# A larger share per slot for background weight preparation in the last three blocks of the first network, and a lower planned price for the scans of the last weight matrix

## The chip, the cores and the metric

The kernel runs on one core of a Trainium2 chip. The metric is the device time of one execution in microseconds (us). The engines are TensorE (PE, matmul; PEld is its weight load), VectorE (DVE), ScalarE (ACT), GpSimd (POOL) and SyncE (SP, which issues the DMAs).

## The reference

A strided-attention layer over 4 batches, 8 heads, 576 positions and head size 64 gives 2304 tokens of width 512. Two feed-forward networks follow; the weights are float64 on the host.

```python
h = x @ w_in                                # 512 -> 2048
x = (h * cos(h)) @ w_out                    # 2048 -> 512
g = x @ w_gate                              # 512 -> 1536
out = (g * sigmoid(g) * (x @ w_val)) @ w_out2   # 1536 -> 512
```

## The kernel before

**Tokens and stages.** The 2304 tokens are cut into five blocks (`BLOCKS`): three of 512 and two of 384, called blocks 0 to 4. After attention the first network runs for all five blocks, then the second.

**First network.** Each block has 16 slots, one for each 128 rows of the 2048, so there are 80 slots, 0 to 79; block 2 begins at slot 32, block 3 at 48, block 4 at 64. In a slot TensorE does `up1` (12 matmuls into one of four PSUM banks of the pool `pm`) and one or two times `down1` (12 matmuls each, for an earlier slot whose product is waiting in a queue). Every operand is split in two float16 halves, high and low, so a product is three matmuls (`mm3`, L491 to L493). The nonlinearity takes five steps, spread over three later slots: `up1_a` (ACT, L524), `up1_b` (DVE, L527), `up1_c` (ACT, L531), `up1_d` (DVE, L534), `up1_e` (ACT L538 and POOL L539). A bank is free again after `up1_d`. All engines run their instructions in the order in which they are written.

**Second network.** There are 30 slots s0 to s29, six for each block. Every slot does seven products for a pair of 128-row pieces (`multiply`, 84 matmuls of 256 columns in blocks 0 to 2), and the previous slot's two `down2` contractions with a tile of `w2` (24 matmuls of 512 columns in blocks 0 to 2). Its nonlinearity uses L602, L608, L609, L613 and L614; its sums L947, L951 and L993, of which L993 (ACT) runs once in a slot. Six 1792 KB weight sets are read back from DRAM in turn (`load_w7`).

**Background work.** The float64 weights must be turned into float32, scanned for their largest value, scaled and split. These steps stand in one queue, `fill`, each with a planned cost in us of VectorE. In every slot of the first network `pump` takes steps from its front for as long as a credit lasts. The slot's budget is what fills the credit, in two halves; urgent pieces for the next block's activations (`pump_urgent`, one per slot) are charged to the same credit.

```python
work = 2.6 * n / 512          # and 2.6 * n / 512 more for each down1 in the slot (n: the slot's, or that down1's, tokens)
budget = (work - 1.25 * n / 512) * (SHARE if blk < SB else SHARE2)
```

The order of the queue from block 2 on is: the scales of `w_gate` and `w_val`; twelve halves of `pair_half` (one for each of the two matrices and each of six pairs: two conversions, four POOL sums at L792, three splits and stores to DRAM); a first pass over the twelve tiles of `w_out2` that only scans them (`scan_later`, L170); their common scale (`top_later`, `scale_later`; L126, then a small matmul at L132 and L133); and a second pass, `in_place_later`, that loads each of the twelve tiles again and makes the tile of `w2`. One such tile is: ACT L220, DVE L227, DVE L231, ACT L241 (high half), DVE L244 (low half), all in the `raw` ring of six 512 KB buffers.

**What happens if the queue isn't empty in time.** In the second network `need(("out2", i))` runs the queue up to tile `i` on the spot, right before the `down2` that reads it. `pump` is also called there twice in a slot, with 2.0 and 3.5.

**A common scale** is a 128-column matmul at L132 in TensorE's own order; it waits for DVE's L126 and the next matmul can wait for the reduction at L133.

Of the kernel before, what the change touches and what calls it, by code (L numbers as in the profile page):

```python
# [57 lines left out]
XM = 3  # L58
HOMES, LATE, UNIT = 24, 4, 16
W7S = 4  # L60
SHARE, SHARE2, SB = 0.95, 0.6, 2


WHERE = [((q, c), (3 + q, c)) if q < 3 else ((6, 0), (6, 256))
# [11 lines left out]
def build(tc, qk_l, qk_s, v_l, v_s, w_in, w_out, w_gate, w_val, w_out2, mask_l, mask_s, eye32, eye16, out):  # L76
    nc = tc.nc
    wide = w_in.dtype != F32
    with ExitStack() as ctx:
# [87 lines left out]
        def scan_raw(mat, i):  # L167
            t = raw[mat, i].popleft()
            src = t.bitcast(F32)[:, :, 1] if wide else t
            nc.vector.tensor_reduce(out=parts_w[mat][:, i:i + 1], in_=src, op=ALU.max, axis=AX.X, apply_absolute_value=True)  # L170
            load_raw()
# [3 lines left out]
        def later(cost, fn, key=None):  # L175
            fill.append((cost, fn, key))
# [71 lines left out]
        def begin(steps):  # L248

            if steps:  # L250
                later(*steps[0])
            while held:
                later(*held.popleft())
            held.extend(steps[1:])
# [21 lines left out]
        def scan_later(mat, j, cost=0.63):  # L276
            later(cost, lambda: scan_raw(mat, j))
# [3 lines left out]
        def top_later(mat):  # L281
            begin([])
            later(0.6, lambda: tops.__setitem__(mat, spread_tops(parts_w[mat], wide)))

        def scale_later(mat, bound):
            later(0.6, lambda: scale_w.__setitem__(mat, common_scale(tops[mat], bound)))
# [14 lines left out]
        def in_place_later(mat, j, tiles):  # L301

            box, steps = conv_steps(mat, j, None, False, lambda: None)

            def last():
                lo_part(tiles[j][:, 1], box["c"], scale_w[mat][0], tiles[j][:, 0])
                load_raw()

            if rests:
                steps.insert(2, rests.popleft())  # L310
            begin(steps + [(0, lambda: hi_part(tiles[j][:, 0], box["c"], scale_w[mat][0]))])
            rests.append((0.7, last, (mat, j)))

        def direct_end():
            begin([])
            while rests:
                later(*rests.popleft())
# [351 lines left out]
        for k in range(len(gs) + LAGS[3] + 1):  # L669
            def group(lag):  # L670
                return gs[k - lag] if 0 <= k - lag < len(gs) else None
            i, g = 2 * (k // 6), k % 6
# [76 lines left out]
        def pair_later(j):  # L749

            last = {}
            for mi, mat in enumerate(("gate", "val")):
                pair_half(j, mi, mat, last)

            def hi():
                last["h"] = unit_free.popleft()
                for mi, mat in enumerate(("gate", "val")):
                    c = slice(256 * mi, 256 * mi + 256)
                    hi_part(homes[last["h"]][:, 0, c], last["f"][:, c], scale_w[mat][0])

            def lo():
                h = homes[last["h"]]
                for mi, mat in enumerate(("gate", "val")):
                    c = slice(256 * mi, 256 * mi + 256)
                    lo_part(h[:, 1, c], last["f"][:, c], scale_w[mat][0], h[:, 0, c])
                unit_free.append(last["i"])
                store_home(j, 6, last["h"])

            begin([(0, hi), (1.0, lo)])
# [40 lines left out]
        def open_weights(lag):  # L810

            if lag + 4 <= UNIT:
                most[0] = UNIT
            if not opened and most[0] == UNIT and max(taken, default=0) < UNIT:
                opened.append(True)
                scale_later("gate", TW_IN)
                scale_later("val", TW_IN)
                for j in range(NPR):
                    pair_later(j)
                begin([])  # L820
                later(0, lambda: None, "pairs")
                for i in range(M2):
                    scan_later("out2", i, 1.7)
                top_later("out2")
            if len(opened) == 1 and lag < LATE and max(taken, default=0) < LATE:
                opened.append(True)
                most[0] = LATE
                for i in range(3):
                    later(1.0, lambda: None)
                scale_later("out2", TW_OUT)  # L830
                for i in range(M2):
                    in_place_later("out2", i, w2)
                direct_end()
# [49 lines left out]
        for blk in range(NBLK):  # L883
            for m in range(M1):
# [21 lines left out]
                if slot >= HEAD:  # L906
                    open_weights(lag)
# [158 lines left out]
```

## Time and profile before

| | |
|---|---|
| median of 3 runs | 958.53 us (955.04 to 970.91) |
| the profiled execution | 956.14 us, span 954.4 us |
| mean granted TensorE clock | 0.968 |
| PE busy | 886.1 us (93%) |
| DVE busy | 596.7 us (63%) |
| ACT busy | 492.2 us (52%) |
| POOL busy | 169.3 us (18%) |
| DMA | 150.94 MB, mean 158 GB/s |

The attention ends at about 105 us, the first network at about 490 us, and the second network has the rest. PE is busy for most of the span, so what counts is where it is not, and where its clock is below 1. The mean shares hide that these places lie close together.

### The profile page before, as it was taken

What the parts mean: (1) busy time and instruction counts of PE and PEld (TensorE: products, weight loads), DVE (VectorE), ACT (ScalarE), POOL (GpSimd) and SP (SyncE); (2) the same over time, 40 slices, a digit from 0 to 9 for tenths busy, and PEclk for the clock granted to TensorE, in tenths of its full rate; (3) what the DMA queues carried; (4) which work ended last, traced back from release to release, by engine and by line L of the source; (5) the groups of instructions that cost most, each with busy time, mean ns of one, the idle gap of its engine ahead of it and who ended that gap; (6) DMA issues with size and microseconds to landing.
All of it is one profiled execution on the core that took longest, in us unless ns stands there. A gap on an engine that the chain in (4) does not pass through costs nothing.

```text
span 954.4 us, 16929 instructions
## 1 busy us (share of the span) xinstructions
PE 886.1 (93%) x6688; PEld 561.6 (59%) x6688; DVE 596.7 (63%) x1161; ACT 492.2 (52%) x1002; POOL 169.3 (18%) x223
## 2 busy tenths in 40 slices
PE   7989998999999999999997777777999999999997
PEld 4667543344444444555665444445777777788886
DVE  4988889784656788785635445544554554555444
ACT  4879889662345567664544333333533443444433
POOL 3434134211133454532220000000000000000000
PEclk7999999899999999999999888888999999999999
DMA  9998813267434554342464332223423523544600
GB/s 295 349 300 256 280 67 104 94 225 260 177 112 154 180 184 146 121 145 76 156 232 165 122 122 100 78 78 122 155 90 144 198 87 145 199 155 172 227 24 34
DMA packets 35391, 150.94 MB, mean 158 GB/s; under 512 B 4240, under 2 KB 5520, under 8 KB 31472
## 3 DMA queue, kind: packets, MB, share of 16 engines
q1 hardware_dynamic: 35312, 149.87, 45.4%
q8 instruction: 52, 0.85, 0.4%
q14 instruction: 27, 0.22, 0.1%
HBM read 134.13 MB, written 15.73 MB: 157 GB/s over the span
## 4 chain that ended last, share of the span: by engine, by line
PE 77%; DVE 7%; ACT 5%; DMA 5%; issue 3%; POOL 2%; SPq 0%; POOLq 0%; ACTq 0%; DVEq 0%
PE bank L491 13%; PE bank L493 13%; PE bank L492 13%; PE acc L493 11%; PE acc L491 11%; PE acc L492 11%; DMA v_pair<-v_s 3%; PE bank L385 2%; PE po L438 2%; ACT arena L241 1%; DMA vl<-v_l 1%; POOL arena L539 1%; DVE arena L244 1%; ACT tb L524 1%; DVE tb L527 1%
## 5 line engine op out<-in xcount | busy, mean ns | idle before, releaser
L491 PE MATMUL acc<-arena 128*128 128x512 f16 (+1 forms) x560 | 206.9, 369 | 41.0 <-ACT arena L241 40.0
L491 PE MATMUL bank<-xs,wi 128*128 128x256 f16 (+3 forms) x736 | 221.1, 300 | 9.3 <-DVE tb L534 4.5
L492 PE MATMUL bank<-xs,wi 128*128 128x256 f16 (+3 forms) x736 | 221.0, 300 | 0.0
L493 PE MATMUL bank<-xs,wi 128*128 128x256 f16 (+3 forms) x736 | 220.8, 300 | 0.0
L493 PE MATMUL acc<-arena 128*128 128x512 f16 (+1 forms) x560 | 206.5, 369 | 0.9 <-DVE arena L244 0.9
L492 PE MATMUL acc<-arena 128*128 128x512 f16 (+1 forms) x560 | 207.0, 370 | 0.3 <-DVE arena L614 0.3
L491 PEld LDWEIGHTS <-arena 128*128 128x128 f16 x952 | 94.4, 99 | 97.4 <-ACT arena L241 44.3
L493 PEld LDWEIGHTS <-arena 128*128 128x128 f16 x952 | 94.2, 99 | 66.7 <-DVE arena L244 8.0
L539 POOL TENSOR_TENSOR arena<-tb,arena 128x512 f16<-128x512 f32 (+1 forms) x80 | 89.1, 1114 | 243.7 <-ACT arena L538 217.1
L951 DVE TENSOR_TENSOR arena<-bank,cv 128x512 f32<-128x512 f32 (+1 forms) x90 | 57.1, 635 | 118.0 <-PE bank L493 117.9
L492 PEld LDWEIGHTS <-arena 128*128 128x128 f16 x952 | 94.4, 99 | 56.6 <-issue 7.3
L492 PEld LDWEIGHTS <-wi 128*128 128x128 f16 x768 | 75.4, 98 | 49.8 <-issue 13.8
L491 PE MATMUL bank<-xs,arena 128*128 128x256 f16 (+1 forms) x392 | 102.4, 261 | 0.0
L492 PE MATMUL bank<-xs,arena 128*128 128x256 f16 (+1 forms) x392 | 102.4, 261 | 0.0
L493 PE MATMUL bank<-xs,arena 128*128 128x256 f16 (+1 forms) x392 | 102.4, 261 | 0.0
L491 PEld LDWEIGHTS <-wi 128*128 128x128 f16 x768 | 75.5, 98 | 40.6 <-issue 3.4
L493 PEld LDWEIGHTS <-wi 128*128 128x128 f16 x768 | 75.3, 98 | 34.8 <-issue 1.1
L613 ACT ACTIVATE arena<-tb 128x512 f16<-128x512 f32 (+1 forms) x60 | 35.2, 587 | 111.4 <-DVE tb L609 111.4
L608 DVE SCALAR_TENSOR_TENSOR tb<-tb,arena 128x512 f32<-128x512 f32 (+1 forms) x60 | 38.0, 633 | 65.0 <-ACT tb L602 65.0
L524 ACT ACTIVATE tb<-bank,quarter,c 128x512 int32<-128x512 f32 (+1 forms) x72 | 52.1, 724 | 48.2 <-PE bank L493 35.9
L602 ACT ACTIVATE tb<-arena,c 128x512 f32<-128x512 f32 (+1 forms) x60 | 40.7, 679 | 69.0 <-DVE arena L951 67.9
L538 ACT ACTIVATE arena<-tb 128x512 f16<-128x512 f32 (+1 forms) x80 | 46.4, 580 | 27.4 <-PE acc L493 26.9
(121 smaller groups left out, 1244.2 us busy)
## 6 DMA issues: line engine op xcount, KB each, us to landing
raw<-w_out SPq DMA_DIRECT2D x56, 512.0 KB, 4.5
wi<-w SPq DMA_DIRECT2D x16, 1792.0 KB, 7.4
arena<-w SPq DMA_DIRECT2D x14, 1792.0 KB, 7.9
raw<-w_gate SPq DMA_DIRECT2D x24, 512.0 KB, 4.5
raw<-w_val SPq DMA_DIRECT2D x24, 512.0 KB, 5.4
w<-arena SPq DMA_DIRECT2D x42, 256.0 KB, 2.0
raw<-w_in SPq DMA_DIRECT2D x16, 512.0 KB
qks<-qk_s SPq DMA_DIRECT2D x8, 594.0 KB, 10.8
```

The source lines that it names most:

```text
L385: nc.tensor.matmul(out=self.sc[r, i, :], lhsT=qk_t[self.i][r, q0:q0 + 64], rhs=qk_t[self.i][r, k0:k0 + w], start=i == 0, stop=False)
L438: nc.tensor.matmul(out=self.po[64 * h:64 * h + 64, i * qn:i * qn + qn], lhsT=v_t[self.i][0:r, t, 64 * h:64 * h + 64], rhs=pt[:, 64 * h:64 ...
L491: nc.tensor.matmul(out=o, lhsT=w[:, 0, c], rhs=x[0], start=first, stop=False, **kw)
L492: nc.tensor.matmul(out=o, lhsT=w[:, 0, c], rhs=x[1], start=False, stop=False, **kw)
L493: nc.tensor.matmul(out=o, lhsT=w[:, 1, c], rhs=x[0], start=False, stop=last, **kw)
L524: nc.scalar.activation(out=c["w"].bitcast(I32), in_=c["ph"], func=AF.Identity, scale=turn[c["blk"]], bias=quarter)
L538: nc.scalar.activation(out=g[:, 0, 0:n], in_=w, func=AF.Copy)
L539: nc.gpsimd.tensor_tensor(out=g[:, 1, 0:n], in0=w, in1=g[:, 0, 0:n], op=ALU.subtract)
L602: nc.scalar.activation(out=t, in_=c["C"][m][:, 0, 0:n], func=AF.Tanh, scale=half[c["blk"]])
L608: nc.vector.scalar_tensor_tensor(out=t, in0=t, scalar=1.0, in1=gate, op0=ALU.add, op1=ALU.mult)
L613: nc.scalar.activation(out=g[:, 0, 0:n], in_=t, func=AF.Copy)
L951: nc.vector.tensor_tensor(out=c["C"][m][:, :, h * right:h * right + h], in0=p, in1=t, op=ALU.add)
```

## The change

Two constants change. `SHARE2`, the share of a slot's budget from block 2 on, goes from 0.6 to 0.7. The planned cost of a scan of `w_out2` goes from 1.7 to 1.0. No instruction is added or removed but for the merging of small neighbours; the background steps are written at other places.

```diff
-SHARE, SHARE2, SB = 0.95, 0.6, 2
+SHARE, SHARE2, SB = 0.95, 0.7, 2
...
-                    scan_later("out2", i, 1.7)
+                    scan_later("out2", i, 1.0)
```

The first place is VectorE at the end of the first network, the last rows before the first L951, which is the first sum of the second network. L170 scans a tile of `w_out2` (`pw_out_83`), L527 and L534 are the steps of a slot. Before:

```order
L170 TENSOR_REDUCE pw_out_83<-raw 128x1
L527 SCALAR_TENSOR_TENSOR tb<-bank,c_4864,tb 128x384
L534 SCALAR_TENSOR_TENSOR tb<-tb,bank 128x384 x2
L138 TENSOR_SCALAR c_5484<-inv_3489,inv_3359 128x1
L138 TENSOR_SCALAR c_5486<-c_5484 128x1
L138 TENSOR_SCALAR c<-inv_3489,inv_3418 128x1
L138 TENSOR_SCALAR c_5490<-c_5484,c 128x1
L951 TENSOR_TENSOR arena<-bank,cv 128x2x256
```

Here a scan, the eleventh of twelve, is the last background step of the first network. The same place now:

```order
L231 SCALAR_TENSOR_TENSOR raw<-raw 128x512
L534 SCALAR_TENSOR_TENSOR tb<-tb,bank 128x384
L244 SCALAR_TENSOR_TENSOR arena<-raw,s_4906,arena 128x512
L527 SCALAR_TENSOR_TENSOR tb<-bank,c_4911,tb 128x384
L534 SCALAR_TENSOR_TENSOR tb<-tb,bank 128x384 x2
L138 TENSOR_SCALAR c_5576<-inv_3497,inv_3359 128x1
L138 TENSOR_SCALAR c_5578<-c_5576 128x1
L138 TENSOR_SCALAR c<-inv_3497,inv_3368 128x1
L138 TENSOR_SCALAR c_5582<-c_5576,c 128x1
L951 TENSOR_TENSOR arena<-bank,cv 128x2x256
```

The low half (L244) of the last tile of `w2` stands before the first L951; all twelve tiles are finished in the first network.

The second place is VectorE in slot s1 and the beginning of s2 of the second network. L608, L609 and L614 are the slot's nonlinearity, L471 a scan of the activations, and L231, L227 and L244 steps of tiles of `w2`. Before:

```order
L608 SCALAR_TENSOR_TENSOR tb<-tb,arena 128x512
L609 SCALAR_TENSOR_TENSOR tb<-tb,arena 128x512
L614 TENSOR_TENSOR arena<-tb,arena 128x512
L231 SCALAR_TENSOR_TENSOR raw<-raw 128x512
L227 TENSOR_SCALAR raw<-raw 128x512
L244 SCALAR_TENSOR_TENSOR arena<-raw,s_5747,arena 128x512
L471 TENSOR_REDUCE parts_4_5573<-xy_70 128x1
L608 SCALAR_TENSOR_TENSOR tb<-tb,arena 128x512
L609 SCALAR_TENSOR_TENSOR tb<-tb,arena 128x512
L951 TENSOR_TENSOR arena<-bank,cv 128x2x256
L614 TENSOR_TENSOR arena<-tb,arena 128x512
```

And now:

```order
L608 SCALAR_TENSOR_TENSOR tb<-tb,arena 128x512
L609 SCALAR_TENSOR_TENSOR tb<-tb,arena 128x512
L614 TENSOR_TENSOR arena<-tb,arena 128x512
L471 TENSOR_REDUCE parts_4_5665<-xy_70 128x1
L608 SCALAR_TENSOR_TENSOR tb<-tb,arena 128x512
L609 SCALAR_TENSOR_TENSOR tb<-tb,arena 128x512
L951 TENSOR_TENSOR arena<-bank,cv 128x2x256
L614 TENSOR_TENSOR arena<-tb,arena 128x512
```

The three steps of a tile of `w2` between the slot's own steps are gone from here, and so they are from every slot up to s6.

The third place is GpSimd in block 2, from the seventh group of four sums L792 (one group per `pair_half`) on; an L539 is the `up1_e` of one slot. Before:

```order
L792 TENSOR_TENSOR arena<-arena 128x256 x4
L539 TENSOR_TENSOR arena<-tb,arena 128x512 x3
L792 TENSOR_TENSOR arena<-arena 128x256 x4
L539 TENSOR_TENSOR arena<-tb,arena 128x512 x3
L792 TENSOR_TENSOR arena<-arena 128x256 x4
L469 MEMSET parts_4_4269 128x1
L539 TENSOR_TENSOR arena<-tb,arena 128x512
L539 TENSOR_TENSOR arena<-tb,arena 128x384
```

And now:

```order
L792 TENSOR_TENSOR arena<-arena 128x256 x4
L539 TENSOR_TENSOR arena<-tb,arena 128x512 x2
L792 TENSOR_TENSOR arena<-arena 128x256 x4
L539 TENSOR_TENSOR arena<-tb,arena 128x512
L792 TENSOR_TENSOR arena<-arena 128x256 x4
L539 TENSOR_TENSOR arena<-tb,arena 128x512 x2
```

The groups stand closer: one or two slots apart where it was three.

## Rows read from the trace of the kernel before

**Rows 1.** Windows: us from:to, length, busy PE, PEld, DVE, ACT, POOL; PEclk, DMA, GB/s.

```profile
105.00:173.00 68.00, 61.82 (x332) 28.46 (x331) 60.59 (x109) 56.53 (x100) 22.69 (x22) 0.95 0.38 127
...
299.90:357.90 58.00, 57.43 (x266) 25.88 (x265) 44.50 (x72) 35.73 (x60) 27.12 (x30) 1.00 0.51 169
...
386.30:425.90 39.60, 39.14 (x242) 23.54 (x241) 31.92 (x64) 27.00 (x50) 15.26 (x19) 1.00 0.40 134
425.90:488.30 62.40, 61.93 (x383) 37.26 (x381) 37.67 (x70) 32.53 (x57) 14.69 (x17) 1.00 0.37 135
...
510.40:656.30 145.90, 104.09 (x641) 64.39 (x640) 72.29 (x136) 50.92 (x83) 0.00 (x0) 0.85 0.29 107
656.30:814.10 157.80, 157.80 (x1190) 116.19 (x1189) 81.58 (x131) 64.02 (x104) 0.00 (x0) 1.00 0.38 137
```

**Rows 2.** Waits of PE from 500 to 660 us: total, times, longest.

```profile
PE acc L491 <- ACT arena L241: 40.0, 12, 5.0
```

**Rows 3.** Timeline of ACT: L993, once per slot, in s0, s6 and s17.

```profile
510.40 0.58 ACT L993 ACTIVATE arena<-bank 128x512 f32<-128x512 f32 x1
...
656.29 0.60 ACT L993 ACTIVATE arena<-bank 128x512 f32<-128x512 f32 x1 [1.89 <-PE bank L493]
...
814.14 0.60 ACT L993 ACTIVATE arena<-bank 128x512 f32<-128x512 f32 x1 [1.22 <-PE bank L493]
```

**Rows 4.** Timeline of slot s1, one wait: start, us, instruction [idle before <-releaser].

```profile
529.86 0.76 ACT L241 ACTIVATE arena<-raw,s 128x512 f16<-128x512 f32 x1 [1.36 <-DVE raw L231]
...
530.68 0.61 PE L491 MATMUL acc<-arena 128*128 128x512 f16 x1 [4.97 <-ACT arena L241]
...
531.09 0.63 PE L492 MATMUL acc<-arena 128*128 128x512 f16 x1
...
535.57 0.27 PE L491 MATMUL bank<-xs,wi 128*128 128x256 f16 x1
...
535.68 0.27 PE L492 MATMUL bank<-xs,wi 128*128 128x256 f16 x1
```

**Rows 5.** Groups by form, DVE, 300 to 490 us: xcount | busy us, mean ns.

```profile
L244 DVE SCALAR_TENSOR_TENSOR arena<-arena,s 128x512 f16<-128x512 f32 x29 | 28.6, 988 | 23.0 <-ACT arena L241 23.0
...
L231 DVE SCALAR_TENSOR_TENSOR arena<-raw,arena 128x512 int32<-128x512 int32 x18 | 13.8, 765 | 0.4
L227 DVE TENSOR_SCALAR arena<-arena 128x512 int32<-128x512 int32 x18 | 9.2, 510 | 0.0
```

**Rows 6.** Groups by form, DVE and ACT, 519 to 650 us.

```profile
L244 DVE SCALAR_TENSOR_TENSOR arena<-raw,s,arena 128x512 f16<-128x512 f32 x12 | 9.0, 751 | 8.0 <-ACT arena L241 8.0
...
L231 DVE SCALAR_TENSOR_TENSOR raw<-raw 128x512 int32<-128x512 int32 x11 | 7.5, 684 | 0.0
L227 DVE TENSOR_SCALAR raw<-raw 128x512 int32<-128x512 int32 x10 | 4.2, 422 | 0.0
...
L241 ACT ACTIVATE arena<-raw,s 128x512 f16<-128x512 f32 x11 | 8.3, 751 | 8.2 <-DVE raw L231 8.2
...
L220 ACT ACTIVATE raw<-raw 128x512 f32<-128x512 f32 x10 | 6.7, 666 | 0.0
```

**Rows 7.** Timeline in slots 41 and 53: PE against ACT's first step.

```profile
317.77 0.38 PE L493 MATMUL bank<-xs,wi 128*128 128x512 f16 x1
...
324.60 0.76 ACT L524 ACTIVATE tb<-bank,quarter,c 128x512 int32<-128x512 f32 x1
...
382.37 0.32 PE L491 MATMUL bank<-xs,wi 128*128 128x384 f16 x1 [1.51 <-DVE q L133]
```

**Rows 8.** Groups by form in 425.9 to 488.3 us, DVE and POOL.

```profile
L170 DVE TENSOR_REDUCE pw_out<-raw 128x1 f32<-128x512 f32 x9 | 6.1, 676 | 0.0
...
L539 POOL TENSOR_TENSOR arena<-tb,arena 128x384 f16<-128x384 f32 x16 | 14.7, 916 | 48.4 <-ACT arena L538 45.4 <-issue 3.0
```

**Rows 9.** Line L170: scans of `w_val`, first and last start.

```profile
L170 DVE TENSOR_REDUCE pw_val<-raw x12: 667/675/682, 224.0 to 254.3; 128x1 f32<-128x512 f32 x12
```

## Prediction

> **What bounds the kernel now.** I read the busy lines and the slices of the page first, then the waits of PE, then cut the span into windows at the stages' ends. PE is the bound almost everywhere: in the windows from 299.9 us on it is busy all but 0.6 of 58.0 us, 0.5 of 39.6 and 0.5 of 62.4, and from 656.3 to 814.1 us without a gap [rows 1]. One stretch breaks this: from 510.4 to 656.3 us PE is busy 104 of 146 us, and its granted clock is 0.85. That is the start of the second network, slots s0 to s6. The reader should see there that PE's waits name one releaser: ACT's L241, 12 times, 40.0 us [rows 2]. L241 makes the high half of a tile of w2, and there are twelve tiles, two per slot. The order has the cause: the queue of background work isn't empty when the second network begins, so each tile is made on the spot, behind the slot's own nonlinearity on DVE and ACT, and PE stands still. In one such wait [rows 4] ACT waits for DVE's L231, then runs 0.76 us, and PE starts after 4.97 us of idling. What follows shows the second loss: the next 512-column matmul starts 0.41 us later, which is the 1.2 GHz level of PE's clock, and some 5 us on the 256-column matmuls start 0.11 us apart, which is 2.4 GHz.
>
> What the stretch costs is read best from L993, which runs once a slot [rows 3]. From s0 to s6 it takes 656.29 - 510.40 = 145.89 us for six slots, 24.3 us each; from s6 to s17, 157.85 us for eleven, 14.35 us each. Both have 512 tokens and the same matmuls. The loss is 145.89 - 6 x 14.35 = 59.8 us: waits and clock together.
>
> **The change part by part.** Both edits move the queue forward. From block 2 on a slot's budget is 7/6 of what it was: with 384 tokens and one down1, (3.9 - 0.94) x 0.6 = 1.78 becomes 2.07 planned us, and each of the twelve scans of w_out2 is charged 1.0 in place of 1.7, 8.4 us less in all. Carried through the 48 slots 32 to 79, the first pass over w_out2 falls in slots 53 to 60 (before, slots 61 to s0), and the second pass in slots 64 to 79. The order confirms the end: the last low half stands before the first L951.
>
> *What goes.* No tile is made in the second network, so slots s1 to s6 contain what s7 to s17 contain, whose 14.35 us I take for them. The weight sets of 1792 KB come one per slot there as they do later, where PE has no gap; the raw loads that shared the queue are gone. The small matmul of the common scale moves too, from s1 to slot 63. The term is -59.8 us. It could be less only by something that s1 to s6 have and later slots don't; that is the scans of block 4 (L471), which the order shows on DVE in both kernels, with DVE at 52% in the undisturbed window [rows 1]. I cost it at nothing.
>
> *What comes, in block 4.* Slots 64 to 79 receive all twelve tiles, and nine scans leave. By DVE's means in the first network a tile is 0.99 + 0.77 + 0.51 = 2.26 us [rows 5], by those in the second 0.75 + 0.68 + 0.42 = 1.86 [rows 6]. DVE was busy 37.7 of 62.4 us there [rows 1]; less nine scans of 0.676 (6.1) [rows 8] and plus twelve tiles it comes to 54 to 59 us, 86 to 94%. ACT gets 12 x (0.75 + 0.67) = 17.0 us more, 49.5 of 62.4, or 79%. PE is still the longest, but the room is small, and every tile hands work DVE to ACT to DVE in queues where the next slot's L527 and L534 stand behind it; PE needs L534 to get its bank back.
>
> Here a page speaks against the change. The means of one tile differ by 0.40 us between the stages, and POOL is what the stages differ in: idle in the second network, busy 14.7 of 62.4 us in this window [rows 1, 5, 6]. The Trainium skill, page "SBUF — State Buffer", section "Who interferes with whom", says that VectorE and GpSimd share a port pair under an exclusive lock, so an instruction of the one can wait for a whole instruction of the other. By that rule at its worst each of a tile's three DVE steps would wait for one L539; what this gives is the second rival. The trace agrees in direction, with a far smaller price.
>
> *What comes, in blocks 2 and 3.* The halves of pair_half move closer. In slots 39 to 47 the planned costs of the steps taken from the queue rise in sum from 22.4 to 27.5 us, which at 2.26 measured for 1.69 planned is 6.8 us of DVE: 44.5 + 6.8 = 51.3 of 58.0, or 88% (before 77%) [rows 1, 5]. The engines are late here already: in slot 41 PE finishes its bank at about 318.2 us, and ACT starts on it at 324.6 [rows 7]. PE lost little by that, because four banks cover it.
>
> No row shows this load with these waits, so the price is bounded. Below, nothing: PE lost 0.46 of 39.6 us, 1.2%, with DVE at 81%. Above, from the stretch 105 to 173 us: DVE at 89%, ACT at 83%, and PE lost 6.2 of 68 us, 9.1% [rows 1]. That stretch is the start of the network and has other losses in it. For both places together, 58.0 + 62.4 = 120.4 us, the ends are 1.4 and 11.0 us. The new load lies nearer to the second row, its cause only partly so; I take 5%, 6.0 us. A common scale that finds DVE late costs PE up to the 1.5 us of slot 53 [rows 7]; a few of these are inside the same range.
>
> *DMA.* Twelve scans in slots 53 to 60 want 12 x 0.524 MB in 8 x 3.9 = 31 us, 202 GB/s. The scans of w_val ran at 12 in 30.3 us, 207 GB/s, with no wait in front of them [rows 9]. Nothing is added.
>
> **Sum.** 956.1 - 59.8 + 6.0 = 902.3 us on the profiled execution, whose 956.1 lies 2.4 us under the median of the runs. I say 903.
>
> **The rivals.**
>
> 1. The first network hides all of it: 956.1 - 59.8 = 896 us. For it: the four banks have covered a lateness of 6 us. Against it: 88 to 94% on an in-order engine. 0.12.
>
> 2. DVE becomes the bound in block 4. At the worst of the lock, three waits of 0.916 us [rows 8] on each of twelve tiles are 33 us: 37.7 - 6.1 + 22.3 + 33 = 86.9 us of DVE work in 62.4, so PE waits 24.5 us; with the 6 us of the sum for the rest, 927 us. For it: 0.99 against 0.75 us on L244. Against it: POOL is busy only a quarter of the time there. 0.15; values between this and the forecast are likelier than its end.
>
> 3. The raw loads come late, because the sets for the second network are issued among them in slots 71 and 78 and take 1792 KB each: a scan or an L220 then holds DVE or ACT. At one wait of 5 us for each set, 912 us. 0.05.
>
> 4. Slower than before: the waits move with the tiles, clock and all. If a tile in block 4 runs the banks out, PE idles, comes back at 1.2 GHz as in slot s1, and pays for every tile what it paid before, 59.8 / 12 = 5.0 us; and if the same happens to each of the sixteen slots of block 4, since a late DVE stays late, the price is 16 x 5.0 = 80 us: 976 us. It decides from the point where DVE's work in a slot exceeds the slot's 3.9 us for many slots in a row. Against it: the highest load that I find is 94%. 0.02.
>
> 5. The change does not empty the queue in time, and need makes the tiles in the second network as before: 956 us. The order excludes it but for a misreading. 0.01.
>
> **How the numbers follow.** Forecast 0.65, rivals 0.12, 0.15, 0.05, 0.02 and 0.01. The forecast's own range is 896 to 912. The range of 893 to 924 takes in the first and third rival and most of the second, and a few us of the spread between runs below. A measurement of this kernel can tell about 2%, 19 us, from no change: faster by more than that means under 939 us. Forecast and rivals 1 to 3 all lie there, 0.97, less 0.01 for a second rival that is worse than its price; rival 5 and that remainder are within 2%; rival 4 is slower: 0.96, 0.02, 0.02.
>
> **What would show it.** Right: L993 at 14.4 us from s0 to s6 and a granted clock of 1.00 there; no wait of PE for L241 in the second network; L244 from raw twelve times before the first L951. DVE at 86 to 94% in block 4, and PE short of busy by 2 to 11 us in blocks 2 to 4. Wrong: any slot of s1 to s6 above 16 us; a granted clock under 0.95 in block 2 to 4; more than 20 us of waits of PE there; a scan that waits for a DMA.

## The result and the profile after

The changed kernel takes 910.03 us (median, 908.77 to 911.48) against 958.22 us: ratio 0.951, 95% interval 0.948 to 0.954, 4.9% faster. The forecast was 903, with 893 to 924 as its range. The profiled execution took 910.15 us, span 908.4 us, mean granted clock 0.981. Times in this document are medians of all runs of a kernel, while the ratios compare means of its undisturbed runs, so that one slow run of the kernel before, 970.91 us, is left out of them.

The windows of the new trace: slots 39 to 41, 42 to 47, 48 to 53 (but for its last 1.1 us, which fall into the next), 54 to 63 and 64 to 79 of the first network, then s0 to s6 and s6 to s17. The columns are those of [rows 1].

```profile
299.40:326.90 27.50, 23.49 (x110) 10.62 (x109) 21.23 (x37) 17.34 (x30) 13.28 (x17) 1.00 0.60 197
326.90:363.10 36.20, 35.61 (x157) 15.65 (x157) 29.02 (x48) 23.79 (x40) 18.88 (x18) 0.95 0.54 179
363.10:398.50 35.40, 28.65 (x140) 14.30 (x139) 30.69 (x56) 21.09 (x37) 16.53 (x20) 0.90 0.49 170
398.50:439.30 40.80, 40.42 (x251) 24.32 (x250) 23.38 (x48) 19.00 (x34) 9.16 (x10) 1.00 0.45 154
439.30:502.80 63.50, 61.90 (x383) 37.26 (x382) 51.12 (x98) 45.74 (x80) 15.91 (x17) 1.00 0.35 129
...
524.90:610.70 85.80, 85.80 (x649) 63.14 (x647) 49.81 (x91) 35.48 (x59) 0.00 (x0) 1.00 0.35 128
610.70:768.00 157.30, 157.30 (x1187) 115.81 (x1185) 82.07 (x133) 64.16 (x106) 0.00 (x0) 1.00 0.39 143
```

The hole at the start of the second network is closed: PE is busy all of 85.8 us, at full clock, where it was busy 104.1 of 145.9 us at 0.85. New holes stand in the first network: 4.0 us in the first window and 6.8 us in the third, with the clock at 0.95 and 0.90 in the second and third.

Slots 48 to 53 have no line in [rows 1]. In the kernel before they are this window, in which PE lost 1.5 us:

```profile
357.90:386.30 28.40, 26.89 (x147) 14.22 (x146) 23.47 (x43) 19.54 (x35) 15.05 (x18) 1.00 0.40 140
```

The waits of PE in the new kernel, from 240 to 500 us (total, times, longest):

```profile
PE bank L491 <- DVE q L133: 11.2, 6, 4.5
PE bank L491 <- DVE tb L534: 2.8, 4, 1.6
```

In the same stretch of the kernel before they were:

```profile
PE bank L491 <- DVE q L133: 3.6, 6, 1.5
PE bank L491 <- DVE tb L534: 0.2, 1, 0.2
```

And from 500 to 660 us, to hold against [rows 2]:

```profile
PE bank L491 <- DVE arena L951: 0.8, 1, 0.8
```

The wait for L241 is gone; the waits for L133 and L534 have grown. Four starts on ACT's timeline measure what each stage gained or lost: L524 of slots 30, 63 and 79 of the first network (one L524 per slot), and L993 of s6 of the second.

```profile
241.32 0.77 ACT L524 ACTIVATE tb<-bank,quarter,c 128x512 int32<-128x512 f32 x1
...
437.54 0.67 ACT L524 ACTIVATE tb<-bank,quarter,c 128x384 int32<-128x384 f32 x1 [0.48 <-PE bank L493]
...
501.81 0.67 ACT L524 ACTIVATE tb<-bank,quarter,c 128x384 int32<-128x384 f32 x1 [0.32 <-PE bank L493]
...
610.66 0.60 ACT L993 ACTIVATE arena<-bank 128x512 f32<-128x512 f32 x1
```

The same starts of the kernel before ([rows 3] has the fourth, 656.29 us):

```profile
241.76 0.77 ACT L524 ACTIVATE tb<-bank,quarter,c 128x512 int32<-128x512 f32 x1
...
424.26 0.67 ACT L524 ACTIVATE tb<-bank,quarter,c 128x384 int32<-128x384 f32 x1 [0.47 <-PE bank L493]
...
487.34 0.67 ACT L524 ACTIVATE tb<-bank,quarter,c 128x384 int32<-128x384 f32 x1 [0.98 <-PE bank L493]
```

The stages between them take, in us:

| stage | before | after | difference |
|---|---|---|---|
| slot 30 to 63 (blocks 2 and 3) | 182.5 | 196.2 | +13.7 |
| slot 63 to 79 (block 4) | 63.1 | 64.3 | +1.2 |
| slot 79 to s6 | 169.0 | 108.9 | -60.1 |

With 0.4 us less before slot 30 and 0.4 us less behind s6 this is the 46.0 us between the spans. The second network gave what was forecast; the first took back 14.9 us, of which nearly all was lost in blocks 2 and 3.

Where in blocks 2 and 3? This is the timeline of the changed kernel round the common scale of slot 41, POOL, ACT, DVE and PE together (its view begins at 322 us, so the first row shows three of POOL's four sums):

```profile
322.33 2.54 POOL L792 TENSOR_TENSOR arena<-arena 128x256 f32<-128x256 f32 x3
...
322.67 0.22 PE L132 MATMUL bank<-tops,ones 128*128 128x128 bf16 x1
...
323.41 2.20 ACT L241 ACTIVATE arena<-arena,s 128x512 f16<-128x512 f32 x4 [1.66 <-POOL arena L792]
324.17 1.91 DVE L244 SCALAR_TENSOR_TENSOR arena<-arena,s 128x512 f16<-128x512 f32 x2 [1.37 <-ACT arena L241]
...
326.00 0.74 DVE L527 SCALAR_TENSOR_TENSOR tb<-bank,c,tb 128x512 f32<-128x512 f32 x1
...
326.66 0.27 DVE L133 TENSOR_REDUCE q<-bank 128x1 f32<-128x128 f32 x1
...
326.99 0.59 PE L491 MATMUL bank<-xs,wi 128*128 128x512 f16 x1 [4.10 <-DVE q L133]
...
327.36 0.63 PE L492 MATMUL bank<-xs,wi 128*128 128x512 f16 x1
327.79 0.63 PE L493 MATMUL bank<-xs,wi 128*128 128x512 f16 x1
...
330.31 0.38 PE L493 MATMUL bank<-xs,wi 128*128 128x512 f16 x1
```

The reader should follow it upward from PE's wait. PE has done the small matmul L132 at 322.67 and could go on with slot 42; but its next bank is the one that L132 has just written (the built program gives both the same PSUM bank), and DVE's L133 must read it first. L133 stands behind the low halves of a pair half and one L527; the low halves wait for ACT, and ACT waits for POOL's four sums. PE stands still for 4.1 us and then runs its 512-column matmuls 0.42 us apart until 330.3, the 1.2 GHz level. At slot 53 it happens again, 4.45 us and slow matmuls until 398.5.

Theory A is drawn from this: what the larger share costs is DVE's lateness, and most of it is charged at the two common scales, with the clock behind them; a tile of w2 that is made ahead of need in the second network is cheap. Against it stood B (a tile costs PE some 5 us wherever it is made in the second network, so both edits are needed) and C (the cost is the load of blocks 2 and 3, whatever the waits are called).

### The profile page after: what moved, and what is told of

Same layout as the page of the kernel before. It is cut to its first block, busy times and chain, and to the rows that moved or that the text cites. A ratio compares the mean times of both kernels' runs of the same rounds, so it can differ in the third digit from the quotient of the medians.

```text
span 908.4 us, 16941 instructions
## 1 busy us (share of the span) xinstructions
PE 873.5 (96%) x6688; PEld 562.2 (62%) x6688; DVE 597.6 (66%) x1161; ACT 492.2 (54%) x1002; POOL 171.2 (19%) x223
## 4 chain that ended last, share of the span: by engine, by line
PE 74%; issue 6%; POOL 5%; DMA 5%; ACT 5%; DVE 5%; SPq 0%; POOLq 0%; ACTq 0%; DVEq 0%
PE bank L491 13%; PE bank L492 13%; PE bank L493 13%; PE acc L492 10%; PE acc L491 10%; PE acc L493 10%; POOL arena L792 3%; DMA vl<-v_l 3%; PE bank L385 2%; POOL arena L539 2%; PE po L438 2%; DMA v_pair<-v_s 1%; ACT tb L524 1%; ACT arena L538 1%; ACT arena L241 1%
## 5 line engine op out<-in xcount | busy, mean ns | idle before, releaser
L491 PE MATMUL acc<-arena 128*128 128x512 f16 (+1 forms) x560 | 200.8, 358 | 1.0 <-ACT arena L613 1.0
L492 PE MATMUL acc<-arena 128*128 128x512 f16 (+1 forms) x560 | 200.8, 358 | 0.3 <-DVE arena L614 0.3
L493 PE MATMUL acc<-arena 128*128 128x512 f16 (+1 forms) x560 | 200.6, 358 | 0.0
L539 POOL TENSOR_TENSOR arena<-tb,arena 128x512 f16<-128x512 f32 (+1 forms) x80 | 90.3, 1129 | 251.0 <-ACT arena L538 215.8
L951 DVE TENSOR_TENSOR arena<-bank,cv 128x512 f32<-128x512 f32 (+1 forms) x90 | 57.2, 636 | 117.5 <-PE bank L493 117.0
L493 PEld LDWEIGHTS <-arena 128*128 128x128 f16 x952 | 93.2, 98 | 57.3 <-issue 0.8
L492 PEld LDWEIGHTS <-arena 128*128 128x128 f16 x952 | 93.2, 98 | 53.6 <-issue 1.6
L491 PEld LDWEIGHTS <-arena 128*128 128x128 f16 x952 | 93.3, 98 | 52.6 <-issue 0.5
L524 ACT ACTIVATE tb<-bank,quarter,c 128x512 int32<-128x512 f32 (+1 forms) x72 | 52.0, 723 | 50.7 <-PE bank L493 39.6
L602 ACT ACTIVATE tb<-arena,c 128x512 f32<-128x512 f32 (+1 forms) x60 | 40.7, 679 | 64.6 <-DVE arena L951 63.5
L608 DVE SCALAR_TENSOR_TENSOR tb<-tb,arena 128x512 f32<-128x512 f32 (+1 forms) x60 | 38.0, 634 | 37.5 <-ACT tb L602 37.4
L538 ACT ACTIVATE arena<-tb 128x512 f16<-128x512 f32 (+1 forms) x80 | 46.4, 580 | 28.9 <-PE acc L493 27.3
```

The lines of the kernel that those rows point to most:

```text
L491: nc.tensor.matmul(out=o, lhsT=w[:, 0, c], rhs=x[0], start=first, stop=False, **kw)
L492: nc.tensor.matmul(out=o, lhsT=w[:, 0, c], rhs=x[1], start=False, stop=False, **kw)
L493: nc.tensor.matmul(out=o, lhsT=w[:, 1, c], rhs=x[0], start=False, stop=last, **kw)
L524: nc.scalar.activation(out=c["w"].bitcast(I32), in_=c["ph"], func=AF.Identity, scale=turn[c["blk"]], bias=quarter)
L538: nc.scalar.activation(out=g[:, 0, 0:n], in_=w, func=AF.Copy)
L539: nc.gpsimd.tensor_tensor(out=g[:, 1, 0:n], in0=w, in1=g[:, 0, 0:n], op=ALU.subtract)
```

## The experiments

Every kernel below is a variation of the changed one. The stage columns are worked out as in the table above; the table stands here and the single runs follow.

| kernel | us | 30 to 63 | 63 to 79 | 79 to s6 |
|---|---|---|---|---|
| before | 958 | 182.5 | 63.1 | 169.0 |
| changed | 910.0 | 196.2 | 64.3 | 108.9 |
| e1_share | 917.4 | 196.2 | 64.0 | 114.6 |
| e2_scan | 906.5 | 182.5 | 63.7 | 116.9 |
| e3_hold | 931.2 | 210.8 | 63.3 | 108.6 |
| e4_scan07 | 903.9 | 182.5 | 63.7 | 116.3 |
| e5_alone | 901.5 | 188.4 | 62.4 | 108.8 |
| e6_late | 908.0 | 189.9 | 68.9 | 107.2 |
| e7_late75 | 908.8 | 189.9 | 64.3 | 108.8 |
| e8_share08 | 917.6 | 204.9 | 61.1 | 108.8 |
| e10_rest7 | 899.9 | 182.5 | 63.4 | 111.0 |

**One edit at a time.** The share alone:

```diff
-                    scan_later("out2", i, 1.0)
+                    scan_later("out2", i, 1.7)
```

> The first edit alone: share 0.7, scans of w_out2 at their old price of 1.7. Worked through the planner, the pair halves lie in the same slots as in the changed kernel (34, 35, 36, 38, 39, 40, 41, 43, 44, 46, 49, 51), seven of the twelve tiles of w2 are made in the first network and five in s0 to s2, each at least two slots before it is read. Theory A (the loss in blocks 2 and 3 comes from the closer halves, that is from the share; the second network only needs tiles made ahead, not all of them): the same gaps of PE at the common scales of slots 41 and 53, and 908 to 914 us. Rival B (both edits are needed, and a tile made in the second network costs PE about 5 us wherever it is made): 5 x 5 = 25 us more than the changed kernel, 935 us.

Measured: 917.43 us, ratio to before 0.960 (0.955 to 0.966). The loss in blocks 2 and 3 is that of the changed kernel to 0.1 us, which A foretold and which puts it on the share. The total missed A's 908 to 914: five tiles in s0 to s2 cost 114.6 - 108.9 = 5.7 us, about 1.1 each, where I had counted on nothing. B's 25 us are excluded.

The scan price alone:

```diff
-SHARE, SHARE2, SB = 0.95, 0.7, 2
+SHARE, SHARE2, SB = 0.95, 0.6, 2
```

> The second edit alone: share 0.6, scans at 1.0. The halves lie as in the kernel before, one tile is made in the first network, eleven in s0 to s5, always one slot ahead of the down2 that reads it. Theory A: no gaps of PE over 2 us in blocks 2 and 3, because the share is old; the second network runs at 14.4 us per slot, since no tile is made on the spot: 896 to 902 us, faster than the changed kernel. Rival B (a tile made in the second network costs 5 us): 11 x 5 = 55 us above 896, 951 us, hardly faster than before.

Measured: 906.50 us, ratio 0.948 (0.945 to 0.950). Blocks 2 and 3 take 182.5 us as before the change. But eleven tiles in the second network cost 8.1 us, and so A's 902 was missed. The waits of PE from 490 to 610 us in this kernel:

```profile
PE bank L491 <- ACT cv L947: 4.7, 5, 1.3
PE bank L132 <- ACT arena L993: 1.9, 1, 1.9
PE bank L491 <- DVE arena L951: 1.2, 1, 1.2
```

These add up to 7.8 us, of which the changed kernel has 0.8: ACT's steps of a tile (L220, L241) stand in front of L947 and L993, which free a bank. In s0, for one, ACT waits 1.69 us for a tile's L231 and then runs L241 and L220, so that L993 starts only at 517.79 us, and PE waits 1.9 us for it. So a tile made ahead of need costs 0.7 to 1.1 us on the average here, and a tile made on the spot cost 5.0 before. Each edit by itself empties the queue early enough that no tile is made on the spot; for the hole in the second network one edit would have done.

**The wait at the common scale.** First I kept the background work away from it:

```diff
+                owed[0] += budget
+                hold = blk >= SB and urgent and urgent[0][0] == 0.6
+                go = 0 if hold else min(owed[0], 1.5 * budget)
+                owed[0] -= go
...
-                pump(budget * 0.5)
+                if go:
+                    pump(go * 0.5)
```

> The changed kernel, with the background work held off in the two slots ahead of each common scale in blocks 2 to 4 and made up for at 1.5 times the budget in the slots after. Theory A (the loss is DVE being late at just the common scale, where the next matmul waits for the reduction L133): no wait for L133 over 2 us, granted clock 1.00 in blocks 2 to 4, 897 to 904 us. Rival C (the loss is the load of blocks 2 and 3 as a whole; what isn't lost at the scale is lost at the banks, through L534): waits for L534 take the place, 906 to 914 us.

Measured: 931.23 us (921.66 to 941.50), ratio 0.970 (0.963 to 0.976), slower than the changed kernel. Its waits of PE from 240 to 530 us:

```profile
PE bank L491 <- DVE tb L534: 15.5, 8, 3.5
PE acc L491 <- ACT xy L507: 3.7, 1, 3.7
PE bank L491 <- DVE q L133: 2.7, 4, 1.5
```

The waits for L133 shrink to those of the kernel before, as A said; but the work that was put off comes at one and a half times the pace, and blocks 2 and 3 lose 28 us, most of it in waits at the banks and in the clock, which was 0.93 from 300 to 380 us. The time lies beyond what A and C had both expected. C is nearer: how densely the halves are written counts by itself. But the run mixes a pause with a faster pace, and can't say what the common scale costs in the changed kernel.

Then I took the small matmul away and left the work where it is:

```diff
-            t, p = bank()[:, 0:128], brief("q")
-            nc.tensor.matmul(out=t, lhsT=ones16, rhs=d, start=True, stop=True)
-            nc.vector.tensor_reduce(out=p, in_=t, op=ALU.max, axis=AX.X)
+            p = brief("q")
+            if alone[0]:
+                nc.vector.tensor_reduce(out=p, in_=d, op=ALU.max, axis=AX.X)
+            else:
...
```

> The changed kernel without the eight small matmuls of the common scales in blocks 2 to 4: DVE reduces the diagonal tile itself, so the maximum over the partitions is left out of those scales; DVE has the same instructions in the same order and the same load. Theory A: no wait for L133, no drop of the granted clock; DVE's lateness of 6 to 8 us stays and shows as waits for L534, 3 to 6 us in all: 898 to 904 us. Rival C (load): the same total wait of PE in blocks 2 and 3 under another name, 907 to 912 us.

Measured: 901.48 us (899.96 to 909.60), ratio 0.944 (0.938 to 0.949). Its waits of PE from 240 to 510 us (five lines were added above, so L539 is L534 of the others):

```profile
PE bank L496 <- DVE tb L539: 7.7, 5, 3.1
PE acc L496 <- ACT xy L512: 0.5, 1, 0.5
```

With the same work in the same order blocks 2 and 3 lose 188.4 - 182.5 = 5.9 us in place of 13.7. So in the changed kernel the common scale's use of a bank, and the clock behind it, cost 7.8 us, and DVE's lateness shows at the ordinary banks in its place. A holds for more than half, C for the rest. Two things limit this. The kernel before has the small matmuls too, and 3.1 us of waits for L133 in blocks 2 and 3; it was not run without them, so the 5.9 us may understate what the lateness costs by up to some 3 us. And A's "no drop of the granted clock" was missed: after a wait of 3.09 us for L539 (at 347.35 us) six matmuls ran 0.42 us apart. The waits were 7.7 us, above the 3 to 6 that I had expected.

**How much share, and where.** Four kernels vary the share or the scans' price:

```diff
# e4_scan07
-SHARE, SHARE2, SB = 0.95, 0.7, 2
+SHARE, SHARE2, SB = 0.95, 0.6, 2
-                    scan_later("out2", i, 1.0)
+                    scan_later("out2", i, 0.7)
# e6_late; e7_late75 has (0.6, 0.75, 0.75)
-                budget = (work - 1.25 * n / 512) * (SHARE if blk < SB else SHARE2)
+                budget = (work - 1.25 * n / 512) * (SHARE if blk < SB else (0.6, 0.7, 0.8)[blk - SB])
-                    scan_later("out2", i, 1.0)
+                    scan_later("out2", i, 0.7)
# e8_share08
-SHARE, SHARE2, SB = 0.95, 0.7, 2
+SHARE, SHARE2, SB = 0.95, 0.8, 2
```

> Share 0.6, scans at 0.7: blocks 2 to 4 as in the kernel before, three tiles of w2 in the first network and nine in s0 to s4, each ahead of need. Theory A' (share costs in blocks 2 and 3, a tile made ahead in the second network costs 0.5 to 1 us, not 5): no gap over 2 us in blocks 2 to 4, slots s0 to s5 between 14.4 and 16 us, 903 to 907 us. Rival (what the scan edit alone lost against 896 us comes from slot s0 and not from the tiles): the same 906 us in spite of the fewer tiles.

Measured: 903.88 us, ratio 0.944 (0.941 to 0.947), in the range of A'. The nine tiles in the second network cost 116.3 - 108.9 = 7.4 us. That is little less than the 8.1 us of the eleven before, so this run does not exclude the rival; the part on s0 below comes back to it.

> Share 0.6 in block 2, 0.7 in block 3 and 0.8 in block 4, scans at 0.7: the halves of block 2 where they were before the change, and yet all twelve tiles in the first network. Theory A': no gap at slot 41, at most one near slot 53, nothing in block 4 although DVE is near its limit there, and 14.4 us per slot from s0 on: 896 to 902 us, the fastest. Rival D (block 4 has no room: DVE becomes the bound there): PE waits for L534 in slots 64 to 79, 905 us or more.

Measured: 907.95 us, ratio 0.948 (0.945 to 0.951). A miss: block 2 is undisturbed, but block 3 loses 7.4 us at a share of 0.7 and block 4 loses 5.8 us at 0.8 (1.7 of them come back before s6). PE's waits from 240 to 500 us show the second common scale again, and a third:

```profile
PE bank L491 <- DVE q L133: 9.4, 6, 4.0
PE bank L132 <- DVE tb L534: 1.0, 2, 0.7
```

So rival D was right at 0.8 on the time, though in block 4 PE waited mostly for L133 and not for L534. That at 0.7 the same block lost only 1.2 us, in the changed kernel, shows how steep it is.

> Share 0.6 in block 2 and 0.75 in blocks 3 and 4, scans at 0.7: as the one before, but with the halves of block 3 closer (49, 51, 53, 56 in place of 49, 51, 54, 57), so that one lies in the slot of the second common scale. Theory A': the gap at slot 53 comes back with its drop of the clock, 2 to 5 us, and the rest is gone: 900 to 905 us. Rival C (load in general): no different from the one before within 1.5 us.

Measured: 908.80 us (903.52 to 912.39), ratio 0.948 (0.944 to 0.953). Block 3 loses 7.4 us, as in the kernel before this one, so where exactly the third and fourth half lie didn't matter; here C was right, and the 900 to 905 us of A' were missed. Block 4 at 0.75 loses 1.2 us.

> The changed kernel with share 0.8 in place of 0.7: halves in slots 34 to 47, the tiles done early in block 4. Theory A' (the share in block 2 is what costs): more and longer gaps in slots 38 to 50, with the clock down after them, 20 to 35 us lost there against 14 at 0.7, and nothing gained behind: 915 to 930 us. Rival (the loss at 0.7 is the accident of two halves meeting two common scales, not load): 905 to 913 us.

Measured: 917.57 us, ratio 0.958 (0.954 to 0.963), with 22.4 us lost in blocks 2 and 3 and 2.0 gained in block 4. Waits of PE from 240 to 512 us:

```profile
PE bank L491 <- DVE tb L534: 8.4, 5, 3.2
PE bank L491 <- DVE q L133: 8.4, 7, 5.0
```

At 0.6, 0.7 and 0.8 blocks 2 and 3 lose 0, 13.7 and 22.4 us. It is no accident of one meeting.

**A version that beats both.** The cheap place for the tiles is block 4 at a share that it bears and the second network from s1 on; s0 is dear: from L524 of slot 79 to L993 of s0 it takes 27.2 or 27.3 us in the three kernels that make tiles in s0 (e1, e2, e4) and 23.1 in the changed one. These 4.1 us are more than half of the 5.7 to 8.1 us that the tiles cost there, so the rival of e4_scan07 was half right:

```diff
# e9_rest (share 0.6 throughout), e10_rest7 (0.7 in block 4 alone); scans at 0.7
-            pump(2.0)
+            if s:
+                pump(2.0)
-            pump(3.5)
+            if s:
+                pump(3.5)
```

> Share 0.6, scans at 0.7, and no background work in s0; three tiles of w2 in the first network, nine in s1 to s6, each ahead of need. Theory A' (blocks 2 to 4 as before the change cost nothing; of the 8 us that the scan edit paid in the second network about half were paid in s0, where ACT is still busy with the end of the first network): nothing lost in blocks 2 to 4, slots s1 to s6 at 15 us, 900 to 903 us. Rival (the tiles cost the same wherever in the second network they are made): 904 us, as with the work in s0.

Measured: 900.12 us (897.28 to 914.07), ratio 0.939 (0.937 to 0.942), some 4 us below e4_scan07, which differs from it in s0 alone: as A' said, though the intervals of the two ratios overlap a little. The trace that is read for the pair is the next kernel's; there s0 comes 22.9 us after slot 79.

> As the one before, with share 0.7 in block 4 alone: six tiles in the first network, six in s1 to s4. Theory A': about 1 us lost in block 4, 2 to 3 us in the second network, 898 to 902 us. Rival D (block 4 has no room above 0.6): 4 us or more lost there and 903 us or more.

Measured: 899.91 us, ratio 0.940 (0.937 to 0.943). Block 4 loses 0.3 us, the second network 2.1 us for six tiles. Waits of PE from 240 to 490 us:

```profile
PE bank L491 <- DVE q L133: 3.7, 6, 1.5
PE bank L491 <- DVE tb L534: 0.2, 1, 0.2
```

They are those of the kernel before the change (3.6 and 0.2 us). Both kernels are some 10 us faster than the changed one, whose own runs beside them follow.

> The changed kernel again, beside the two others on the same chip: 908 to 912 us, with the two gaps of over 4 us at the common scales of slots 41 and 53. If the gaps were an accident of one execution, they are missing here and the loss in blocks 2 and 3 is under 10 us.

Measured: 910.00 us (908.10 to 911.45), ratio 0.951 (0.948 to 0.953); L133 11.2 us again, longest 4.5, and 13.8 us lost from slot 30 to 63. The gaps are a property of the program.

## Why the prediction was right, and which term was not

*The hole in the second network, -59.8 us.* Measured -60.1 us. The waits for L241 are gone, the clock is 1.00, and s0 to s6 take 14.3 us each. Reading the loss from L993's spacing, waits and clock in one number, was the step that carried the forecast.

*That nothing is special about s1 to s6.* Right: PE is busy without a gap there.

*Block 4.* The forecast was 86 to 94% for DVE, and PE was to lose a few us. DVE was busy 51.1 of 63.5 us, 81%, and the stage took 1.2 us more. The load came out lower mainly because I added durations of instructions to the busy time of a window. Neighbouring instructions overlap: DVE's groups in this window add up to 58.0 us where its busy time is 51.1 (before the change, to 41.9 where it is 37.7). In durations DVE got 16.1 us more, the low end of the 16.2 to 21.0 that I had added. The tile's steps, by these groups:

```profile
L231 DVE SCALAR_TENSOR_TENSOR raw<-raw 128x512 int32<-128x512 int32 x11 | 9.4, 858 | 0.0
L244 DVE SCALAR_TENSOR_TENSOR arena<-raw,s,arena 128x512 f16<-128x512 f32 x11 | 8.4, 765 | 8.1 <-ACT arena L241 8.0
...
L227 DVE TENSOR_SCALAR raw<-raw 128x512 int32<-128x512 int32 x12 | 6.1, 506 | 3.1 <-ACT raw L220 3.1
```

That is 2.13 us per tile, between my 1.86 and 2.26. The splits of the activations beside them, L244 from wi, fell from 0.96 to 0.74 us as they no longer met POOL. The second rival, the lock at its worst, did not happen: a tile's price rose by 0.27 us over the second network's, not by 2.75 (three times 0.916). The Trainium skill's rule on the shared port pair (page "SBUF — State Buffer", section "Who interferes with whom") is in agreement with the direction for L231 and L227; L244 is hardly touched. Single instructions show more: the L231 at 481.04 us starts 0.07 us after an L539 of 0.91 us and takes 1.39 us, where one that meets no POOL instruction takes 0.68. So a wait near the size that I had priced (0.916 us) does occur, but few of the steps meet an L539 so.

*Blocks 2 and 3: the mis-sized term.* I put 6.0 us on slots 39 to 47 and block 4 together, as 5% between two rows of DVE load. By the windows these two took 5.7 and 1.1 us more, close to the 6.0. But slots 48 to 53, which lie between the windows of [rows 1], got no term, and they took 36.5 us in place of 28.4, 8.1 more: of 14.9 us lost, more than half was at a place that I had not priced. The row for it was there. In the kernel before PE lost 1.5 of 28.4 us in these slots, with DVE at 83%, and [rows 7] shows that very wait for L133.

The load itself was forecast well in the place that I looked at (50.3 us of DVE work in slots 39 to 47, forecast 51.3). In slots 48 to 53 DVE now has some 31 us of work, more than the 28.4 us which these slots took before. So load is likely a part of the cause; but nearly the same load costs 7.8 us less without the small matmuls. The rest is a chain of hand-offs, POOL's sums to ACT's L241 to DVE's L244, in front of an instruction on which PE waits. I had named that ("a common scale that finds DVE late costs PE up to the 1.5 us of slot 53; a few of these are inside the same range") and taken the largest wait of the old trace as its limit: leaving slots 48 to 53 without a price and that limit are the step that failed. The waits were 4.1 and 4.5 us, and the clock fell behind both: 8 matmuls ran 0.42 us apart in place of 0.216, some 1.6 us, and 17 ran 0.32 apart in place of 0.16, some 2.6 us. Waits of 14.0 us less the 3.8 of the kernel before, plus 4.2 of clock, make 14.4 of the 14.9 us. That slots 39 to 47 and block 4 came close to their 6.0 us is luck in part, since in the first of them it was one such gap with its clock and not a loss spread over the load.

Of the signs that I had named, the granted clock fell under 0.95 in one stretch (0.90 from 363.1 to 398.5 us), and PE was short of busy by 13.3 us in slots 39 to 79, above the 11 at the end of my range.

*DMA.* No scan waited: DVE's L170 has no idle time in front of it in the new trace either. The third rival fell. (The 207 GB/s of the forecast took twelve loads for the time between the first and the twelfth start; over eleven spacings it is 190, below the 202 that it was to cover.)

*The rivals of both signs.* Slower than before was far off; so was no effect. The first rival, 896 us, would have been the changed kernel with blocks 2 and 3 undisturbed, and the last kernels come within 4 us of it.

## What to carry to other kernels

When background work is moved off a hole, price every stretch that it moves into, and not by the load of the engine that takes it alone: look at the instructions for which the bound engine waits, and first at the one that it waits for with the shortest lead, here the reduction after a helper's small matmul that takes a buffer of the main ring. A wait that the old trace shows as 1.5 us is no limit for it, since it grows with the lateness in front of it. And when a change has two parts that push the same way, try each alone: here the second part, alone and a little stronger, gained 6 us more than both, and 10 with one dear slot spared.

## What was not expected of the hardware

After PE's waits of 4.10 and 4.45 us its matmuls ran at 1.2 GHz for 3.3 us (326.99 to 330.31) and 5.4 us (393.06 to 398.46); after waits of 1.60 and 1.62 us they did not. This added 1.6 and 2.6 us to the two long waits. The length of one wait does not decide it alone: after 3.09 us in e5_alone and 3.15 us in e3_hold the matmuls ran at 1.2 GHz for 2.5 and 3.6 us, and after 3.54 us in e3_hold (at 359.77 us) they ran at 2.4 GHz at once.

The first 30 slots are the same in all these kernels, and the first step of slot 0 began at 108.2 us in one profiled execution and at 115.6 in another. This stage, and not the part under study, may make much of the spread within a kernel's runs; that isn't shown, as only one execution of each kernel has a trace. A few us are told apart best by starts within one trace, which is why the stages are compared from slot 30 on.
